# Block loads for k of chunk 2, v loaded and cast through GpSimd's queue, preparation ordered by tensor

## The chip, the cores and the metric

The kernel runs on one core of a Trainium2 chip. The metric is the time of one execution on the device, in microseconds; where several runs were made, their median is given. The core's engines are TensorE (PE, matrix products, with a weight load beside each), VectorE (DVE), ScalarE (ACT), GpSimd (POOL) and SyncE (SP). SP, ACT and GpSimd also issue DMA transfers, each through a queue of its own.

## What is computed

A retention layer (a linear recurrence with one decay per head) feeds a feed-forward layer with a tanh GELU:

```python
def _attn_ref(q, k, v):                       # B, H, S, D = 4, 8, 768, 64
    gamma = 1.0 - 2.0 ** (-5.0 - np.arange(H))
    state = zeros(B, H, D, D)
    for t in range(S):
        state = gamma * state + k[t] (outer) v[t]
        y[t] = (1/sqrt(D)) * q[t] @ state

def reference(q, k, v, moe_w_in, moe_w_out):
    x = attn_out.transpose(0, 2, 1, 3).reshape(B * S, H * D)   # 3072 x 512
    h = x @ w_in                                               # 512 x 2048
    return gelu_tanh(h) @ w_out                                # 3072 x 512
```

All inputs and the output are float32. The kernel computes in float16 with float32 accumulation.

## The kernel before

The sequence of 768 steps is cut into 6 chunks of 128, numbered 0 to 5. Within a chunk the recurrence becomes three matrix products for each of the 4 batches: scores (`mm_A`, k against q, masked by `ev_A`), the output inside the chunk (`mm_yi`, v against the masked scores) and the output from the state that the earlier chunks left (`mm_yc`). A fourth product, `mm_s`, makes the chunk's contribution to the state; `ev_S` adds it to the decayed state, and `decay` (on GpSimd) prepares the next decayed copy. The transposed result is copied to `xT` and feeds the feed-forward part of the same chunk: `moe1` (16 units with GELU on ScalarE), then `moe2` (4 batches of 4 units each, `units2`), whose results go out by `ev_O`.

**Order.** The order of the instructions on every engine is the order in which the program writes them; nothing reorders them. `run(units, after)` writes the units of TensorE work one after another and, after the unit of a given number, the extra calls listed under that number. So the attention work of chunk c+1 is threaded between the feed-forward units of chunk c. The phases from chunk 1 on are: `moe2` of chunk 0 with the transposes and scores of chunk 1; `moe1` of chunk 1 in halves (16 units) with loads, preparation and transposes of chunk 2; `moe2` of chunk 1; then a loop over c = 2, 3, 4 with one list of 32 units each, in which chunk n = c + 1 is prepared; at last chunk 5 alone.

**Loads and preparation.** `load(c)` writes the loads of a chunk to SP's queue. A tensor is loaded in one of two ways. `load1` (L102) brings 128 x 512 float32 of one batch with time on the partitions, in rows of 256 bytes. `load_blk` (L114) brings a tensor of all four batches in 16 DMAs of 64 KB with rows of 128 bytes, placed so that a transposition of each 32 x 32 block is all that is missing. `prep1` (L185, L188) multiplies q or k by its decay factors, or casts v; `prep_blk` (L199) does the same for the block form. `prep(c, b)` writes all of these for one batch to GpSimd.

**Transposes.** The scores need q and k with the head dimension on the partitions. What was loaded in block form is transposed by VectorE, 32 x 32 at a time (L251). The rest is transposed by TensorE against an identity matrix into PSUM (`mm_T`, L242) and copied to SBUF by `ev_T` (L226). Which tensor of which chunk takes which way is set by `BLK`: q from chunk 2 on, k from chunk 3 on. k also keeps its ordinary form, since `mm_s` needs it.

**Buffers.** Pools of tiles go round: a new tile takes the oldest buffer of its tag, and its first writer waits until the earlier readers are done. q's raw block tile has two buffers, that of k one (`kT32`); raw k and v have six each, the prepared block k (`kT16`) two.

A TensorE unit of `moe1` or `moe2` in the later phases is 4 matmuls. DMA issues by SP, ACT and GpSimd appear in the profile as DMA_DIRECT2D.

Of the kernel before, what the change touches and what calls it, by code (L numbers as in the profile page):

```python
# [9 lines left out]
F16 = mybir.dt.float16  # L10
F32 = mybir.dt.float32
# [5 lines left out]
def kernel(  # L17
# [9 lines left out]
    nc = tc.nc  # L27
    B, H, S, Dh = q.shape
    C = 128
    NCk = S // C  # L30
    NHP = H // 2
# [27 lines left out]
    ld = ctx.enter_context(tc.tile_pool(name="ld", bufs=2 * B))  # L59
    pre = ctx.enter_context(tc.tile_pool(name="pre", bufs=2 * B))  # L60
    att = ctx.enter_context(tc.tile_pool(name="att", bufs=4))
# [13 lines left out]
    raw = {}  # L75
# [1 line left out]

    BLK = {"q": (2, 3, 4, 5), "k": (3, 4, 5)}  # L80

    def ld_all(key):
        if key not in raw:
            raw[key] = ld.tile(
                [128, B * NHP, 4, 32],
                F32,
                tag=key[0],
                bufs=2 if key[0] == "q32" else 1,
                name=key[0],
            )  # L90
        return raw[key]

    def ld_tile(nm, c, b):
        if nm == "q":
            t = ld_all(("q32", c)).rearrange("p (b hp) a d -> p b (hp a d)", b=B)
            return t[:, b].rearrange("p (h d) -> p h d", h=H)
        if (nm, c, b) not in raw:
            raw[nm, c, b] = ld.tile([128, H, Dh], F32, tag=f"{nm}32", bufs=6, name=f"{nm}32")
        return raw[nm, c, b]

    def load1(eng, nm, c, b):
        eng.dma_start(  # L102
            out=ld_tile(nm, c, b),
            in_=srcs[nm][b, :, c * C:(c + 1) * C, :].rearrange("h p d -> p h d"),
        )

    def load_blk(nm, c):
        t = ld_all((nm + ("32" if nm == "q" else "T32"), c))
        src = srcs[nm].rearrange("b (hp j) s (dd d) -> j dd s (b hp) d", j=2, dd=2)
        for j in range(2):  # L110
            for dd in range(2):
                for a in range(4):
                    p0, t0 = (2 * j + dd) * 32, c * C + a * 32
                    nc.sync.dma_start(  # L114
                        out=t[p0:p0 + 32, :, a, :], in_=src[j, dd, t0:t0 + 32]
                    )

    def load(c):
        for nm in "qk":
            if c in BLK[nm]:  # L120
                load_blk(nm, c)
        for b in range(B):
            for nm in "vk" if c in BLK["k"] else "kv":
                load1(nc.sync, nm, c, b)

    def hold(nm, c, b, until):

# [18 lines left out]
        out=misc[:, 0:1], in_=zero[:, 0:1], func=AF.Gelu_apprx_tanh, scale=1.0  # L146
# [16 lines left out]
    for j in range(2):  # L163
        for hp in range(NHP):
            nc.vector.tensor_scalar(
                out=mask[:, j, hp],
# [6 lines left out]
    h16 = {}  # L173
    blk16 = {}

    def prep1(eng, nm, c, b):
        t = pre.tile(
            [128, H, Dh], F16, tag=f"{nm}16", bufs=6 if nm == "q" else 2 * B, name=f"{nm}16"
        )
        src = ld_tile(nm, c, b)  # L180
        if nm == "v":
            if eng is nc.scalar:
                eng.copy(out=t, in_=src)  # L183
            else:
                eng.tensor_copy(out=t, in_=src)  # L185
        else:
            col = OQ if nm == "q" else OK
            eng.tensor_tensor(  # L188
                out=t,
                in0=src,  # L190
                in1=cst[:, col:col + H].unsqueeze(2).broadcast_to([128, H, Dh]),
                op=ALU.mult,
            )
        h16[nm, c, b] = t

    def prep_blk(nm, c, b):
        key, tag, col = ("q32", "q16", OQT) if nm == "q" else ("kT32", "kT16", OKT)
        t = pre.tile([128, NHP * 4, 32], F16, tag=tag, bufs=6 if nm == "q" else 2, name=tag)
        nc.gpsimd.tensor_tensor(  # L199
            out=t,  # L200
            in0=ld_all((key, c))[:, b * NHP:(b + 1) * NHP].rearrange("p hp a d -> p (hp a) d"),
            in1=cst[:, col:col + 16].unsqueeze(2).broadcast_to([128, 16, 32]),
            op=ALU.mult,
        )
        blk16[nm, c, b] = t

    def prep(c, b):
        for nm in "qk":
            if c in BLK[nm]:
                prep_blk(nm, c, b)  # L210
        prep1(nc.gpsimd, "k", c, b)
        prep1(nc.gpsimd, "v", c, b)

    def pair(t, hp):
        return t[:, 2 * hp:2 * hp + 2]

    qkT = {}
    a_sb = {}
    xT = {}
    pss = {}  # L220

    def copy_on(eng, out, in_):
        if eng is nc.scalar:
            eng.copy(out=out, in_=in_)  # L224
        else:
            eng.tensor_copy(out=out, in_=in_)  # L226
# [5 lines left out]
    def bank(tag, dt=F32, shape=(128, NHP, 128), name="ps"):  # L232
        return psum.tile(list(shape), dt, tag=tag, bufs=BANKS[tag], name=name)

    def mm_T(c, b):
        parts = [(i, nm) for i, nm in enumerate("qk") if c not in BLK[nm]]
        if not parts:
            return
        ps = bank("att", F16, (128, 2, NHP, 128), "qkT_ps")
        for i, nm in parts:  # L240
            for hp in range(NHP):
                nc.tensor.transpose(  # L242
                    out=ps[:, i, hp], in_=pair(h16[nm, c, b], hp), identity=iden
                )
        pss["T", c, b] = ps

    def ev_T(c, b, eng=nc.vector):
        t = att.tile([128, 2, NHP, 128], F16, tag="qkT", name="qkT")
        for i, nm in enumerate("qk"):
            if c in BLK[nm]:  # L250
                nc.vector.transpose(  # L251
                    out=t[:, i].rearrange("p hp t -> p (hp t)"),
                    in_=blk16.pop((nm, c, b)).rearrange("p ha d -> p (ha d)"),
                )
        if ("T", c, b) in pss:
            i0 = sum(c in BLK[nm] for nm in "qk")
            copy_on(eng, t[:, i0:], pss.pop(("T", c, b))[:, i0:])
        qkT[c, b] = t

    def mm_A(c, b):  # L260
        t = qkT[c, b]
# [90 lines left out]
    def att_T(c, *bs):  # L352
        for b in bs:
            mm_T(c, b)
            ev_T(c, b)
# [73 lines left out]
    def moe1(c, fc):  # L429
        h_ps = bank("h", shape=(128, B * C), name="h_ps")  # L430
        moe1_mm(c, fc, h_ps, 0, B * C)
        gelu(g_tile(c, fc)[:, fc % 2], h_ps)
# [55 lines left out]
    def run(units, after):  # L488
        for i, u in enumerate(units):
            u()  # L490
            for f, *args in after.get(i, ()):
                f(*args)

    VE, AC, PO, SY = nc.vector, nc.scalar, nc.gpsimd, nc.sync
# [88 lines left out]
    def units2(c, b, n=4, tag="o"):  # L583
        u = [(lambda i=i: moe2(c, b, range(i, i + n), tag)) for i in range(0, NF, n)]
        last = u[-1]
        u[-1] = lambda: (last(), ev_O(c, b))
        return u
# [30 lines left out]


    load(2)  # L620
    for b in range(B):
        prep(2, b)
    run(
        [
            (lambda fp=fp, t=t: moe1_two(1, fp, *t))
# [2 lines left out]
        ],  # L628
        {
            1: [(att_AY, 1, (2,), "o", 1, (3,), VE)],  # L630
            3: [(att_S, 1, 2)],
            4: [(att_AY, 1, (3,), "o", 1, (), VE)],
            6: [(att_S, 1, 3)],
            8: [(att_T, 2, 0), (load, 3)],
            10: [(att_T, 2, 1)],
            12: [(att_AY, 1, (), "o", 2, (0, 1), None)],
            14: [(att_T, 2, 2)],
            15: [(att_T, 2, 3)],
        },
    )  # L640
    run(
        [x for b in range(B) for x in units2(1, b)],
        {
            2: [(att_AY, 2, (0, 1), "h", 2, (2, 3), AC)],
            4: [(att_S, 2, 0)],
            5: [(att_S, 2, 1)],
            8: [(att_AY, 2, (2, 3), "h", 2, (), AC)],
            10: [(att_S, 2, 2)],
            11: [(att_S, 2, 3)],
        },  # L650
    )


    for c in range(2, NCk - 1):
        n = c + 1
        after = {
            2: [(prep, n, 0)],
            4: [(prep, n, 1)],
            6: [(prep, n, 2), (att_T, n, 0)],
            8: [(prep, n, 3), (att_T, n, 1)],  # L660
            9: [(load, n + 1)] if n + 1 < NCk else [],
            12: [(att_AY, n, (), "att", n, (0, 1), None)],
            13: [(att_T, n, 2)],
            15: [(att_T, n, 3)],
            18: [(att_AY, n, (0, 1), "h", n, (2, 3), VE)],
            20: [(att_S, n, 0)],
            21: [(att_S, n, 1)],
            25: [(att_AY, n, (2, 3), "h", n, (), AC)],
            27: [(att_S, n, 2)],
            28: [(att_S, n, 3)],  # L670
        }
        run(
            [(lambda fc=fc: moe1(c, fc)) for fc in range(NF)]
            + [x for b in range(B) for x in units2(c, b)],
            after,
        )
    c = NCk - 1
# [36 lines left out]
```

## Time and profile before

| | |
|---|---|
| time, median of 10 runs | 217.9 us (216.68 to 218.16) |
| the profiled execution's own time | 218.05 us |
| its span, first to last instruction | 215.8 us |
| TensorE busy | 207.4 us (96%) |
| VectorE, ScalarE, GpSimd busy | 82.8, 87.2, 96.9 us |
| mean granted TensorE clock | 0.996 |
| DMA | 124417 packets, 32.88 MB, mean 152 GB/s |
| block loads of q, of kT | 64 and 48 DMAs of 64 KB, 2.8 and 2.7 us from issue to landing |
| k and v loads on SP | 22 and 18 DMAs of 256 KB, 4.6 and 4.3 us to landing |

The profile is of one execution. "Busy" counts an engine's own work and not its DMA issues by SP or its waits. Groups and waits are named by line number, engine, and the tiles written and read; a wait names the waiter, then who released it. Times within the execution are counted from the start of the span.

### The profile page before, as it was taken

The page shows a single profiled execution, that of the slowest core. Times are in us where ns is not written, and L with a number is a line of the kernel's source. Part 1 is how long each engine was busy: PE and PEld are TensorE (multiplying, and loading weights), DVE is VectorE, ACT ScalarE, POOL GpSimd, SP SyncE. Part 2 cuts the span into 40 slices and gives each one's busy share as a digit, 9 for nine tenths or more (in the row PEclk, how much of TensorE's full clock was granted, in tenths as well). Part 3 has the DMA queues.
Part 4 walks back from the last instruction along what each step waited for, and adds up shares of the span by engine and source line. Part 5 has one row for each costly group of instructions (what it writes and reads, how often), then busy time and mean ns, then how long its engine had stood idle before and what let it go on. Part 6 is the DMA issues. An engine that isn't in the chain of part 4 may idle for free.

```text
span 215.8 us, 3912 instructions
## 1 busy us (share of the span) xinstructions
PE 207.4 (96%) x1544; PEld 113.0 (52%) x1544; DVE 82.8 (38%) x152; ACT 87.2 (40%) x150; POOL 96.9 (45%) x116
## 2 busy tenths in 40 slices
PE   7889999999979999999999999999999999999993
PEld 2447644457867655444545444545444545444462
DVE  3445200198635562153691343682344650100001
ACT  2584562254444233276223275223366123476120
POOL 3599200324169542699433799412399321100000
PEclk9999999999999999999999999999999999999998
DMA  7999999997899789997679975589900012100111
GB/s 175 288 249 207 206 204 241 214 319 124 178 226 199 111 156 185 248 256 124 103 145 257 280 130 88 81 160 248 290 2 3 0 49 87 62 0 0 52 75 71
DMA packets 124417, 32.88 MB, mean 152 GB/s; under 512 B 118064, under 2 KB 122544, under 8 KB 124400
## 3 DMA queue, kind: packets, MB, share of 16 engines
q1 hardware_dynamic: 107984, 20.58, 48.3%
q0 software_dynamic: 5584, 8.65, 17.1%
q10 hardware_dynamic: 10832, 3.41, 6.5%
q8 instruction: 12, 0.20, 0.4%
q14 instruction: 5, 0.04, 0.1%
HBM read 30.53 MB, written 6.29 MB: 171 GB/s over the span
## 4 chain that ended last, share of the span: by engine, by line
PE 68%; DMA 15%; SPq 9%; POOL 5%; issue 1%; DVE 0%; ACT 0%
PE o_ps L445 32%; PE h_ps L412 28%; DMA w_out<-in_moe_w_out_dram 7%; DMA k<-in_k_dram 6%; SPq L102 5%; SPq L114 4%; PE y_ps L300 2%; PE a_ps L265 2%; POOL k L188 2%; PE y_ps L287 2%; DMA v<-in_v_dram 2%; PE s_ps L319 1%; POOL w_in L393 1%; POOL q L199 1%; POOL w_out L402 1%
## 5 line engine op out<-in xcount | busy, mean ns | idle before, releaser
L445 PE MATMUL o_ps<-w_out,g 128*128 128x512 f16 (+1 forms) x400 | 88.1, 371 | 0.0
L412 PE MATMUL h_ps<-xT,w_in 128*128 128x512 f16 (+2 forms) x488 | 86.6, 334 | 0.5 <-ACT g L427 0.5
L427 ACT ACTIVATE g<-h_ps 128x512 f16<-128x512 f32 (+1 forms) x98 | 57.4, 588 | 51.7 <-PE h_ps L412 51.7
L412 PEld LDWEIGHTS <-w_in 128*128 128x128 f16 x488 | 45.7, 98 | 37.0 <-issue 0.7
L445 PEld LDWEIGHTS <-g 128*128 128x128 f16 x400 | 37.7, 98 | 38.8
L278 DVE TENSOR_TENSOR a_sb<-a_ps,mask 128x512 f16<-128x512 f32 x48 | 30.1, 684 | 19.6 <-PE a_ps L265 19.5
L188 POOL TENSOR_TENSOR k<-k,cst 128x512 f16<-128x512 f32 x24 | 25.1, 1047 | 16.7 <-DMA k<-in_k_dram 16.7
L470 POOL DMA_DIRECT2D out_dram<-o_sb x17 | 9.7, 568 | 46.4 <-ACT o_sb L465 36.8
L465 ACT COPY o_sb<-o_ps 128x512 f32<-128x512 f32 x19 | 11.1, 585 | 42.5 <-PE o_ps L445 33.8
L345 POOL TENSOR_TENSOR stg<-st,cst 128x512 f32<-128x512 f16 x16 | 16.4, 1045 | 10.3 <-DVE st L336 9.3
L336 DVE TENSOR_TENSOR st<-s_ps,stg 64x256 f16<-64x256 f32 x32 | 13.5, 421 | 17.8 <-PE s_ps L319 17.2
L199 POOL TENSOR_TENSOR q<-q,cst 128x512 f16<-128x512 f32 x16 | 16.7, 1042 | 5.8 <-DMA v<-in_v_dram 5.8
L251 DVE STREAM_TRANSPOSE qkT<-q 128x512 f16<-128x512 f16 x16 | 11.2, 700 | 13.1 <-POOL q L199 13.1
L224 ACT CAST xT<-y_ps 128x512 f16<-128x512 f32 x15 | 8.3, 588 | 13.0 <-PE y_ps L300 12.9
L199 POOL TENSOR_TENSOR kT<-kT,cst 128x512 f16<-128x512 f32 x12 | 12.5, 1042 | 0.0
L188 DVE TENSOR_TENSOR q<-q,cst 128x512 f16<-128x512 f32 x7 | 4.8, 686 | 18.7 <-DMA q<-in_q_dram 18.7
L152 PE MATMUL spin_ps<-zero 128*128 128x512 f16 x32 | 10.4, 467 | 1.2 <-DVE zero L144 1.2
L482 DVE COPY o_sb<-o_ps 128x256 f32<-128x256 f32 x1 | 0.4, 424 | 25.2 <-PE o_ps L445 25.2
L185 POOL CAST v<-v 128x512 f16<-128x512 f32 x16 | 9.6, 601 | 0.0
L183 ACT CAST v<-v 128x512 f16<-128x512 f32 x8 | 5.0, 621 | 10.0 <-issue 7.7
L251 DVE STREAM_TRANSPOSE qkT<-kT 128x512 f16<-128x512 f16 x12 | 8.3, 690 | 1.7 <-POOL kT L199 1.7
L226 DVE CAST xT<-y_ps 128x512 f16<-128x512 f32 x9 | 5.9, 687 | 7.8 <-PE y_ps L300 7.8
(33 smaller groups left out, 97.1 us busy)
## 6 DMA issues: line engine op xcount, KB each, us to landing
k<-in_k_dram SPq DMA_DIRECT2D x22, 256.0 KB, 4.6
v<-in_v_dram SPq DMA_DIRECT2D x18, 256.0 KB, 4.3
out_dram<-o_sb POOLq DMA_DIRECT2D x17, 256.0 KB, 3.3
q<-in_q_dram SPq DMA_DIRECT2D x64, 64.0 KB, 2.8
kT<-in_k_dram SPq DMA_DIRECT2D x48, 64.0 KB, 2.7
w_in<-in_moe_w_in_dram POOLq DMA_DIRECT2D x4, 512.0 KB, 9.2
w_out<-in_moe_w_out_dram POOLq DMA_DIRECT2D x4, 512.0 KB, 14.6
v<-in_v_dram ACTq DMA_DIRECT2D x6, 256.0 KB, 5.9
```

What stands on the lines that cost most here:

```text
L102: eng.dma_start(out=ld_tile(nm, c, b), in_=srcs[nm][b, :, c * C:(c + 1) * C, :].rearrange("h p d -> p h d"),)
L152: nc.tensor.matmul(out=ps, lhsT=zero[:, 0:128], rhs=zero, start=True, stop=True)
L188: eng.tensor_tensor(out=t, in0=src, in1=cst[:, col:col + H].unsqueeze(2).broadcast_to([128, H, Dh]), op=ALU.mult,)
L199: nc.gpsimd.tensor_tensor(out=t, in0=ld_all((key, c))[:, b * NHP:(b + 1) * NHP].rearrange("p hp a d -> p (hp a) d"), in1=cst[:, col:col + ...
L251: nc.vector.transpose(out=t[:, i].rearrange("p hp t -> p (hp t)"), in_=blk16.pop((nm, c, b)).rearrange("p ha d -> p (ha d)"),)
L278: nc.vector.tensor_tensor(out=s, in0=ps[j], in1=mask[:, j], op=ALU.mult)
L336: eng.tensor_tensor(out=st[sl, :, b, sl], in0=s_ps[sl, :, sl], in1=stg[sl, :, b, sl], op=ALU.add,)
L345: nc.gpsimd.tensor_tensor(out=stg[:, :, b], in0=st[:, :, b], in1=cst[:, OG:OG + NHP].unsqueeze(2).broadcast_to([128, NHP, 128]), op=ALU.mult,)
L412: nc.tensor.matmul(out=out, lhsT=w_in_sb[wi][:, kc, wr * 128:(wr + 1) * 128], rhs=xT[c][:, kc, t0:t1], start=(kc == 0), stop=(kc == NHP - ...
L427: nc.scalar.activation(out=out, in_=in_, func=AF.Gelu_apprx_tanh, scale=1.0)
L445: nc.tensor.matmul(out=ps[:, n0:n1], lhsT=g_sb[c, fc // 2][:, fc % 2, b * C:(b + 1) * C], rhs=w_out_sb[fc // (NF // NO)][:, fc % (NF // NO ...
L465: nc.scalar.copy(out=o_sb, in_=ps)
```

## The change

- k of chunk 2 is loaded in block form too (`BLK`), so no chunk from 2 on is transposed by TensorE. `mm_T` and `ev_T` keep only the form for chunks 0 and 1.
- v of chunks 2 to 5 is no longer loaded as float32 by SP and cast by an instruction on GpSimd. `load_v` issues a DMA from GpSimd's queue that casts to float16 and writes the `v16` tile.
- `load` now issues q's blocks, kT's blocks, and then k in ordinary form, which is not loaded (or prepared) for the last chunk, whose state nobody needs.
- The raw block tiles of q and k have two buffers each; raw k and v have four.
- `prep` takes a tensor and a list of batches: `"Q"` and `"K"` for the block forms, `"k"` for the ordinary one. `tr` writes the VectorE transposes of one tensor. The calls are placed tensor by tensor, where before they were placed batch by batch.
- In the phase of `moe1` of chunk 1, the scores of chunk 2 for batches 0 and 1 move from its unit 12 to unit 3 of the next phase, those for batches 2 and 3 from unit 2 to unit 6 of that phase, and what follows moves by three units.

```diff
-    BLK = {"q": (2, 3, 4, 5), "k": (3, 4, 5)}
+    BLK = {"q": (2, 3, 4, 5), "k": (2, 3, 4, 5)}
...
-                bufs=2 if key[0] == "q32" else 1,
+                bufs=2,
...
-            raw[nm, c, b] = ld.tile([128, H, Dh], F32, tag=f"{nm}32", bufs=6, name=f"{nm}32")
+            raw[nm, c, b] = ld.tile([128, H, Dh], F32, tag=f"{nm}32", bufs=4, name=f"{nm}32")
...
         for nm in "qk":
             if c in BLK[nm]:
                 load_blk(nm, c)
+        if c + 1 < NCk:
+            for b in range(B):
+                load1(nc.sync, "k", c, b)
+
+    def load_v(c):
+
         for b in range(B):
-            for nm in "vk" if c in BLK["k"] else "kv":
-                load1(nc.sync, nm, c, b)
+            t = h16["v", c, b] = pre.tile([128, H, Dh], F16, tag="v16", bufs=2 * B, name="v16")
+            nc.gpsimd.dma_start(
+                out=t, in_=v[b, :, c * C:(c + 1) * C, :].rearrange("h p d -> p h d")
+            )
...
-    def prep(c, b):
-        for nm in "qk":
-            if c in BLK[nm]:
-                prep_blk(nm, c, b)
-        prep1(nc.gpsimd, "k", c, b)
-        prep1(nc.gpsimd, "v", c, b)
+    def prep(c, nm, *bs):
+
+        for b in bs:
+            if nm in "QK":
+                prep_blk(nm.lower(), c, b)
+            else:
+                prep1(nc.gpsimd, nm, c, b)
...
+    def tr(c, nm, *bs):
+        for b in bs:
+            if (c, b) not in qkT:
+                qkT[c, b] = att.tile([128, 2, NHP, 128], F16, tag="qkT", name="qkT")
+            nc.vector.transpose(
+                out=qkT[c, b][:, "qk".index(nm)].rearrange("p hp t -> p (hp t)"),
+                in_=blk16.pop((nm, c, b)).rearrange("p ha d -> p (ha d)"),
+            )
...
     load(2)
-    for b in range(B):
-        prep(2, b)
+    load_v(2)
     run(
...
             1: [(att_AY, 1, (2,), "o", 1, (3,), VE)],
-            3: [(att_S, 1, 2)],
+            3: [(att_S, 1, 2), (prep, 2, "Q", 0, 1, 2, 3)],
             4: [(att_AY, 1, (3,), "o", 1, (), VE)],
-            6: [(att_S, 1, 3)],
-            8: [(att_T, 2, 0), (load, 3)],
-            10: [(att_T, 2, 1)],
-            12: [(att_AY, 1, (), "o", 2, (0, 1), None)],
-            14: [(att_T, 2, 2)],
-            15: [(att_T, 2, 3)],
+            6: [(att_S, 1, 3), (tr, 2, "q", 0, 1, 2, 3)],
         },
     )
+    prep(2, "K", 0, 1, 2, 3)
+    prep(2, "k", 0, 1, 2, 3)
+    load(3)
+    load_v(3)
     run(
         [x for b in range(B) for x in units2(1, b)],
         {
-            2: [(att_AY, 2, (0, 1), "h", 2, (2, 3), AC)],
-            4: [(att_S, 2, 0)],
-            5: [(att_S, 2, 1)],
-            8: [(att_AY, 2, (2, 3), "h", 2, (), AC)],
-            10: [(att_S, 2, 2)],
-            11: [(att_S, 2, 3)],
+            2: [(tr, 2, "k", 0, 1)],
+            3: [(att_AY, 2, (), "att", 2, (0, 1), None), (tr, 2, "k", 2, 3)],
+            6: [(att_AY, 2, (0, 1), "h", 2, (2, 3), AC)],
+            8: [(att_S, 2, 0)],
+            9: [(att_S, 2, 1)],
+            11: [(att_AY, 2, (2, 3), "h", 2, (), AC)],
+            13: [(att_S, 2, 2)],
+            14: [(att_S, 2, 3)],
         },
     )
...
     for c in range(2, NCk - 1):
         n = c + 1
+        more = n + 1 < NCk
         after = {
-            2: [(prep, n, 0)],
-            4: [(prep, n, 1)],
-            6: [(prep, n, 2), (att_T, n, 0)],
-            8: [(prep, n, 3), (att_T, n, 1)],
-            9: [(load, n + 1)] if n + 1 < NCk else [],
+            1: [(prep, n, "Q", 0, 1, 2, 3), (tr, n, "q", 0, 1)],
+            6: [(prep, n, "K", 0, 1, 2, 3), (tr, n, "k", 0, 1), (tr, n, "q", 2, 3)],
+            10: [(prep, n, "k", 0, 1, 2, 3)] if n + 1 < NCk else [],
+            11: [(load, n + 1), (load_v, n + 1)] if more else [],
             12: [(att_AY, n, (), "att", n, (0, 1), None)],
-            13: [(att_T, n, 2)],
-            15: [(att_T, n, 3)],
+            13: [(tr, n, "k", 2, 3)],
             18: [(att_AY, n, (0, 1), "h", n, (2, 3), VE)],
```

## The prediction

> **What bounds the kernel now.** I read the busy table first, then the waits, the chain of waits, and the timelines of the engines around the one place where they point.
>
> ```profile
> span 215.8 us, 3912 instructions
> PE 207.4 (96%) x1544; PEld 113.0 (52%) x1544; DVE 82.8 (38%) x152; ACT 87.2 (40%) x150; POOL 96.9 (45%) x116
> ```
>
> TensorE sets the time: 96% busy, and no other engine reaches half. Only what it executes or waits for counts. Its largest wait (waiter, releaser, total, times, longest):
>
> ```profile
> PE qkT_ps L242 <- POOL k L188: 1.6, 2, 1.1
> ```
>
> That is 1.6 us in two stalls, in transposes of k that wait for GpSimd. The TensorE timeline puts both at chunk 2:
>
> ```profile
> 60.02 1.91 PE L412 MATMUL h_ps<-xT,w_in 128*128 128x256 f16 x16
> 63.07 0.40 PE L242 MATMUL qkT_ps<-iden,k 128*128 128x128 f16 x4 [1.14 <-POOL k L188]
> 63.30 1.91 PE L412 MATMUL h_ps<-xT,w_in 128*128 128x256 f16 x16
> 65.63 0.40 PE L242 MATMUL qkT_ps<-iden,k 128*128 128x128 f16 x4 [0.42 <-POOL k L188]
> ...
> 67.70 0.62 PE L265 MATMUL a_ps<-qkT 64*128 64x128 f16 x16
> ```
>
> TensorE stood from 61.93 to 63.07 and 0.42 us before 65.63. After 71.33 the chain runs on TensorE to the end with no such piece. What those stalls wait for, in the chain of waits:
>
> ```profile
> 57.50 3.47 DMA v<-in_v_dram
> 60.96 1.05 POOL q L199
> 62.01 1.00 POOL k L188
> ```
>
> and SP's own timeline:
>
> ```profile
> 46.12 10.80 SPq L114 DMA_DIRECT2D q<-in_q_dram  x16
> 56.96 0.49 SPq L102 DMA_DIRECT2D k<-in_k_dram  x1
> ...
> 74.85 9.21 SPq L114 DMA_DIRECT2D kT<-in_k_dram  x16
> ```
>
> Columns: start, duration, what. SP issues the 16 block loads of q, then k and v; they land; GpSimd prepares q, k, v of batch 0, and TensorE transposes. So the ground is SP's queue and the DMA engines. The last line prices 16 block loads: 0.58 us each.
>
> **What the Trainium skill says.** "DMA: Bandwidth & Descriptors", "Issuing engines are not separate DMA queues": transfers started by SP, ACT and GpSimd run on the same 16 DMA engines and interleave, so moving v to GpSimd's queue saves SP's issue time, not transfer time. The trace fits: mean DMA share is 0.93 from 57 to 64 us and 1.16 from 64 to 66, with all of it on SP's queue. Same page, "SWDGE vs HWDGE vs iDMA": a cast during a DMA needs GpSimd's queue, whose descriptors software writes. "SBUF — State Buffer", "Who interferes with whom": vector operations in a two-port mode lock GpSimd's descriptor writing out. Here the vector work beside the new loads is st, xT and a_sb out of PSUM or transposes at 0.69 us, which is the one-element-per-cycle pace of the same engine's other 512-wide work; the trace of before shows no such block.
>
> **The change, part by part.** All times are on the profiled execution (218.05 us, its span 215.8, so 2.25 around it); the median shown is 217.9, so a difference in the span is applied to 217.9.
>
> (a) Removed on TensorE: the 16 transposes of chunk 2's k. Each group of four costs the step from its start to the next work: 63.07 to 63.30, 65.63 to 65.86, 70.01 to 70.24, 71.11 to 71.33: 0.91 us. With them go the two stalls, 1.14 + 0.42 = 1.56. Together 2.47 us, all on the path: the most that this change can give.
>
> (b) Vector engine: four copies out of PSUM (0.40) become four transposes (0.69): +1.2 us, on an engine 38% busy; hidden, but see (e).
>
> (c) GpSimd: per chunk four v casts (4 x 0.60 = 2.4 us) become four DMA issues. A 128-row out issue takes 0.57, a 512-row weight issue 0.80; a v load has 1024 rows of 256 B, so the straight line through both gives an estimate of 1.1 us, 4.4 for four. Bounds: 0.57 if rows cost nothing; above, see rival 2. Chunk 2 also gains four kT preparations (4 x 1.04), chunk 5 loses its four k ones. In each 32 us chunk GpSimd then has 4.2 + 4.2 + 4.2 (q, kT, k), 4.4 (v), 2.3 (outs), 4.2 (decay): 23.5 us, so it keeps up.
>
> (d) SP: in the load of chunk 2, four v loads go and 16 block loads of kT come right behind q's, ahead of k. From 56.96, at 0.53 each (as SP issued them from 51 to 53 us), the last is issued by 65.4; landing 2.6 us after an issue near 64.9: 67.5. That is the best case. But the v loads, issued on GpSimd from 55.2 (its decay of 54.16 ends there) to 59.6, share the DMA engines. SP's k and v loads went at 8 in 8.25 us with the engines full, so v is about 4.1 us of all 16. The 19 block loads in that stretch take 0.27 us each (pace 0.53 at a share of 0.5, 51 to 53 us) to 0.41 (0.58 at 0.7, 72 to 78 us), 5.1 to 7.8 us. Sum 9 to 12 us in the 12 us from 55.2: nearly full. From 46.12 to 50.70, with other transfers ahead, SP managed only five block loads, 0.92 each. At that pace for all 16 and 4.8 us to land (the slowest kT), the last lands at about 75.6: the worst case. I take issue finished at 67.2 (1.8 us beyond the best), last issue at 66.7, and 3.5 us to land (the last two of q took 3.1 and 4.1): L = 70.2.
>
> (e) The new wait. Scores of chunk 2 (L265 before) now need the vector transposes of kT: L, two preparations (2.03), transpose (0.75 with its handover), 0.1 for semaphores: batch 1 can start at L + 2.87. TensorE gets there at 61.93 + 7 units of moe1 (1.75 per two, 6.13) + 4 units of moe2 (0.865, 3.46) = 71.5, and batch 1's scores 0.27 later, 71.77. The stall is L - 68.9, so 1.3 us. Queued behind it is everything on TensorE. Next, batches 2 and 3: the vector engine does four a_sb (2.45) and only then their two transposes (1.35); TensorE needs the last one 3 units + 0.45 + 0.27 after its scores, that is some 0.3 us too early: another 0.3 lost. GpSimd's third kT preparation waits for the first transpose (two buffers), which is done by then.
>
> (f) Further down. k of chunk 2 follows kT on SP: issued by 71.5, landed by about 76, prepared behind kT at 77 to 78.5, used by the first state update at about 79.8: hidden by about 4 us (first batch ready by 75.5). Chunk 3: SP then has 16 + 16 blocks, 71.5 + 9.6 + 9.2 + 1.5 (v of chunk 3 beside them) = 91.8, landed 94.5, scores possible at 97.4; TensorE gets there at about 88 + 13 units (11.2) = 99. Cover 1.7 us; from chunk 4 on SP is a whole chunk ahead, since the second kT buffer removes its waits. Preparing by tensor puts q and kT first (8.3 us after GpSimd is free at about 89), against scores 11 us into the chunk: hidden. The v16 and k32 buffers that the loads wait for are free long before.
>
> Sum: -2.47 + 1.3 + 0.3 = -0.87 us: 217.9 becomes **217.0 us**.
>
> **Rivals.** *1. The transfer is hidden anyway.* If the last kT lands before 68.9, only the 0.3 stays: -2.17, 215.7. For it: the DMA share leaves room on paper (9 of 12 us), and SP itself is the pacer at 0.53. Against it: landings stretch to 4.0 to 4.5 us whenever 256 KB loads run beside blocks, as at the end of chunk 3's kT.
>
> *2. GpSimd becomes the bound (slower).* The v issues stand ahead of q's and kT's preparation: 55.2 + 4t + one decay + four q + one decay + two kT + the transpose = 64.3 + 4t against 71.77. It decides from t = 1.9, eats the whole gain of 2.17 at t = 2.4, and at t = 3.1 ("SBUF — State Buffer", "A bandwidth-pool intuition that's wrong (but worth ruling out)", gives about 3100 ns for such a DMA beside a vector copy, 620 alone; taking it as the issue is an estimate) the scores start at 76.7: a stall of 4.9, +2.7, 220.6. Against it: issues in this trace never passed 0.93 us. For it: none has 1024 rows, nor a cast with rows that short.
>
> *3. The two queues share badly.* If v's packets get more than half of the engines, kT lands at 71.7 or later: a stall of 2.8, +0.6 or more; at 73, +1.9, 219.8. Break-even is L = 71.07.
>
> *4. Chunk 3 is late too.* If its blocks land 2.5 us later than I put them, its scores stall 0.8: -0.1, 217.8. That the transposes stay on TensorE is excluded by the code.
>
> **How the numbers follow.** A run of this kernel varies by about 0.3% (0.65 us), so less than that is called the same. Forecast, L from 69.0 to 71.4: 0.50, of which 0.33 is faster by more than 0.65 (L below 70.4) and 0.17 within it. Rival 1: 0.17, faster. Rival 2: 0.12, slower. Rival 3: 0.12, of which 0.03 same. Rival 4: 0.09, of which 0.07 same and 0.02 slower. That gives faster 0.50, same 0.27, slower 0.23. The range from 215.8 to 219.0 leaves out part of rival 1's lower end and the heavier ends of rivals 2 and 3, about 2 in 10; the forecast's own range is 215.8 to 218.2.
>
> **What would show it.** Right: no L242 work for chunk 2 and its two stalls gone; a wait of 1 to 2 us of the scores on the vector transpose of kT near 72, a smaller one some 4 us later; v issues on GpSimd of about 1.1 us; kT of chunk 2 issued until about 67. Wrong: issues of 2 us or more; block loads at 0.9 us each to the end; a wait at chunk 3's scores near 99; or TensorE work apart from chunk 2 that grew.

## The result

The changed kernel is slower: 219.44 us in the median of 14 runs (217.79 to 220.99) against 217.73 us of the kernel before (51 runs, 216.43 to 218.55). The ratio over these runs is 1.0086, with a 95% interval from 1.0067 to 1.0104 (that of the two medians alone is 1.0079). The forecast was 217.0 us, in a range from 215.8 to 219.0. Executions more than 1.5% above the fastest of their kernel are left out as slow, here and below: one of the changed kernel (222.09 us) and three of a later one.

The profiled execution of the changed kernel took 219.45 us, 1.40 more than that of before (218.05), and its span is 1.9 us longer. The head of its page:

```profile
span 217.7 us, 3866 instructions
PE 206.3 (95%) x1528; PEld 112.1 (51%) x1528; DVE 84.2 (39%) x152; ACT 87.0 (40%) x150; POOL 102.2 (47%) x116
```

TensorE has 16 matmuls fewer and 1.1 us less to do, as meant, and yet the span grew: TensorE waits more than it saves. The waits of the changed kernel (waiter, releaser, total, times, longest) say for what:

```profile
PE a_ps L271 <- DVE qkT L261: 3.1, 3, 1.9
```

The two stalls of the transposes of k, 1.6 us, are gone. Three new ones, 3.1 us, stand at the scores, which wait for VectorE's transposes of kT. TensorE's timeline (start, duration, work, and in brackets the idle time ahead) has two of these waits at chunk 2 and the third at chunk 3:

```profile
73.42 0.40 PE L271 MATMUL a_ps<-qkT 64*128 64x128 f16 x8 [1.92 <-DVE qkT L261]
74.43 0.40 PE L271 MATMUL a_ps<-qkT 64*128 64x128 f16 x8 [0.61 <-DVE qkT L261]
...
88.85 11.39 PE L418 MATMUL h_ps<-xT,w_in 128*128 128x512 f16 x52
100.31 0.40 PE L271 MATMUL a_ps<-qkT 64*128 64x128 f16 x8
101.31 0.40 PE L271 MATMUL a_ps<-qkT 64*128 64x128 f16 x8 [0.61 <-DVE qkT L261]
101.64 2.55 PE L418 MATMUL h_ps<-xT,w_in 128*128 128x512 f16 x11
```

and the same two places in the kernel before:

```profile
88.83 11.39 PE L412 MATMUL h_ps<-xT,w_in 128*128 128x512 f16 x52
...
100.70 2.76 PE L412 MATMUL h_ps<-xT,w_in 128*128 128x512 f16 x12
```

Two readings settle where the time went. At 88.85 against 88.83 the changed kernel is exactly level: the saved 2.47 us have been paid back by 1.92 + 0.61 = 2.53 us of waiting. At 101.64 against 100.70 it is 0.94 us behind; 0.61 of that is shown as a wait of the second half of the scores. Nothing of size follows: the last block of `moe2` starts at 199.11 us against 198.02, 1.09 later, and takes 14.02 us in both. What is left of the longer span is its tail, the landing of the last output (2.6 us against 2.0), far from anything that the change touches.

What the scores waited for is seen in GpSimd's and SP's timelines. GpSimd:

```profile
55.16 3.56 POOL L130 DMA_DIRECT2D v<-in_v_dram  x4
...
71.57 4.07 POOL L207 TENSOR_TENSOR kT<-kT,cst 128x512 f16<-128x512 f32 x4 [4.57 <-DMA k<-in_k_dram]
...
79.58 3.57 POOL L130 DMA_DIRECT2D v<-in_v_dram  x4
...
98.46 4.06 POOL L207 TENSOR_TENSOR kT<-kT,cst 128x512 f16<-128x512 f32 x4 [3.68 <-DMA kT<-in_k_dram]
```

SP:

```profile
57.09 11.76 SPq L114 DMA_DIRECT2D kT<-in_k_dram  x16
...
82.42 13.55 SPq L114 DMA_DIRECT2D kT<-in_k_dram  x16
```

GpSimd stood idle for 4.57 and 3.68 us for want of kT. It was free; the data was not there. (The releaser given for the first is a k load that landed at about that time; by the code the instruction needs kT.) The 16 block loads of kT took SP 11.76 us in chunk 2, 0.74 each, and 13.55 in chunk 3, 0.85 each, where those of chunk 3 took 9.21 before, 0.58 each. In both chunks they began before GpSimd had issued the last of its four v loads. A table by stretches, from 60 to 63 us (PE, PEld, DVE, ACT and POOL busy, the clock, the mean DMA share, GB/s), first after the change, then before:

```profile
60.00:63.00 3.00, 3.00 (x32) 2.69 (x30) 0.84 (x2) 1.94 (x4) 1.06 (x2) 1.00 2.06 161
```

```profile
60.00:63.00 3.00, 1.93 (x20) 1.49 (x17) 1.56 (x3) 1.78 (x3) 2.04 (x3) 1.00 0.87 198
```

The share more than doubles, from 0.87 to 2.06, while the GB/s fall from 198 to 161. The two stretches carry different loads (k and v in rows of 256 bytes before; blocks and v, counted by its written float16 bytes, after), so the lines say no more than this: the share counts how long packets last, not how much the engines move. It passes 1 also where only SP's queue is at work, as the prediction noted (1.16 from 64 to 66 us before).

How SP's pace changes is plainer. The four v loads of chunk 2 land between 60.26 and 64.22 us. Up to 64.11 us SP gets seven blocks of kT out in 6.97 us, 1.00 each; the nine after that take 4.74 us, 0.53 each. In chunk 3 the v loads have landed at 88.46, and the blocks come back to 0.53 only from 92.30 on; stores of the output run beside them there too, so not all of that chunk's delay need be v's.

### The profile page after: what moved, and what is told of

Its sections match the earlier page's. It is cut to its first block, busy times and chain, and to the rows that moved or that the text cites. A ratio compares the mean times of both kernels' runs of the same rounds, so it can differ in the third digit from the quotient of the medians.

```text
span 217.7 us, 3866 instructions
## 1 busy us (share of the span) xinstructions
PE 206.3 (95%) x1528; PEld 112.1 (51%) x1528; DVE 84.2 (39%) x152; ACT 87.0 (40%) x150; POOL 102.2 (47%) x116
## 3 DMA queue, kind: packets, MB, share of 16 engines
q10 hardware_dynamic: 10832, 3.41, 6.5%
## 4 chain that ended last, share of the span: by engine, by line
PE 51%; SPq 25%; DMA 14%; POOL 4%; issue 3%; DVE 0%; ACT 0%; POOLq 0%
PE o_ps L451 26%; PE h_ps L418 20%; SPq L114 19%; DMA w_out<-in_moe_w_out_dram 7%; SPq L102 6%; DMA k<-in_k_dram 6%; PE y_ps L306 2%; PE a_ps L271 1%; DMA kT<-in_k_dram 1%; PE y_ps L293 1%; POOL w_in L399 1%; PE s_ps L325 1%; POOL k L196 1%; POOL kT L207 1%; POOL w_out L408 1%
## 5 line engine op out<-in xcount | busy, mean ns | idle before, releaser
L476 POOL DMA_DIRECT2D out_dram<-o_sb x17 | 9.7, 574 | 40.5 <-ACT o_sb L471 32.7
L196 POOL TENSOR_TENSOR k<-k,cst 128x512 f16<-128x512 f32 x20 | 20.7, 1050 | 16.7 <-DMA k<-in_k_dram 16.7
L207 POOL TENSOR_TENSOR kT<-kT,cst 128x512 f16<-128x512 f32 x16 | 16.2, 1043 | 8.2 <-DMA k<-in_k_dram 4.6
L261 DVE STREAM_TRANSPOSE qkT<-kT 128x512 f16<-128x512 f16 x16 | 10.9, 697 | 17.7 <-POOL kT L207 17.7
L207 POOL TENSOR_TENSOR q<-q,cst 128x512 f16<-128x512 f32 x16 | 16.2, 1049 | 2.2 <-DMA kT<-in_k_dram 2.1
L130 POOL DMA_DIRECT2D v<-in_v_dram x16 | 14.3, 912 | 0.0
L233 ACT CAST xT<-y_ps 128x512 f16<-128x512 f32 x15 | 8.3, 588 | 14.3 <-PE y_ps L306 14.2
L271 PE MATMUL a_ps<-qkT 64*128 64x128 f16 x192 | 8.5, 218 | 3.7 <-DVE qkT L261 3.1
L160 PE MATMUL spin_ps<-zero 128*128 128x512 f16 x32 | 9.9, 448 | 1.2 <-DVE zero L152 1.2
```

The lines of the kernel that those rows point to most:

```text
L130: nc.gpsimd.dma_start(out=t, in_=v[b, :, c * C:(c + 1) * C, :].rearrange("h p d -> p h d"))
L196: eng.tensor_tensor(out=t, in0=src, in1=cst[:, col:col + H].unsqueeze(2).broadcast_to([128, H, Dh]), op=ALU.mult,)
L207: nc.gpsimd.tensor_tensor(out=t, in0=ld_all((key, c))[:, b * NHP:(b + 1) * NHP].rearrange("p hp a d -> p (hp a) d"), in1=cst[:, col:col + ...
L261: nc.vector.transpose(out=qkT[c, b][:, "qk".index(nm)].rearrange("p hp t -> p (hp t)"), in_=blk16.pop((nm, c, b)).rearrange("p ha d -> p ( ...
```

## The experiments

Three theories of why the blocks of kT come late were to be told apart. A: the casting load through GpSimd's queue is itself what is heavy. B: any v transfer that runs beside the blocks holds them back by about what it takes itself, whoever issues it and in whatever form. C: SP's own 16 further blocks are what is late, and v has no part. For A speaks the list of DMA queues (packets, MB, share of 16 engines' span):

```profile
q0 software_dynamic: 22224, 10.75, 31.6%
```

Before it is 5584 packets, 8.65 MB and 17.1%. The v loads add 16640 packets of 128 written bytes, which last (0.316 x 217.7 - 0.171 x 215.8) x 16 = 510 us in sum, 31 ns each. That is 2.0 us of all 16 engines per load, 8 per chunk, twice the 4.1 that the prediction took.

**v as float32 through ACT's queue, cast by GpSimd**

```diff
 def load_v(c):  # the calls are spread over ACT's work
-    nc.gpsimd.dma_start(out=t, in_=v[b, :, ...])      # t: float16
+    load1(nc.scalar, "v", c, b)                       # float32, 8 buffers
 ...
+    (prep, 2, "v", 0, 1, 2, 3)                        # casts, behind prep of q (chunk 2), of kT (later)
```

> The changed kernel, but v of chunks 2 to 5 comes as float32 through ACT's queue at about the times at which GpSimd's queue issued it, and GpSimd casts it by instruction. Theory A (the v loads that cast cost the DMA engines about 31 ns a packet where an ordinary 256-byte packet costs 15 to 20, and that slows the block loads of kT): block loads of chunk 2 are issued by about 67 us instead of 68.9, the wait of chunk 2's scores falls from 2.5 to about 1.2 us, the wait of chunk 3's scores (0.9) goes, and the time is about 217.0 (0.3% below the kernel before). Theory B (any second queue beside SP's block loads slows them as much, cast or not): nothing changes, 219.4. Theory C (SP's own queue with 16 more block loads is what is late, v has no part): also 219.4, with block loads at the same pace.

Measured: 228.62 us, ratio 1.051 (1.0445 to 1.0576). A miss for all theories, and of little use for telling them apart. SP's waits show why:

```profile
SPq L114 <- DMA v<-in_v_dram: 32.7, 10, 8.4
```

SP's block loads waited 32.7 us for v loads that ACT issues between its other work, so the 16 blocks of q of chunk 3 took SP 19.50 us. Two queues that were meant to be apart hung together through the waits that the program puts ahead of a DMA: a block of q went out at 57.53 us, when the v load that ACT had issued at 54.11 had landed (57.51). Where v was not in the way, the blocks of kT of chunk 2 went out in 8.51 us, 0.53 each: the pace without company.

**v as float32 through GpSimd's queue, cast by GpSimd**

```diff
-    nc.gpsimd.dma_start(out=t, in_=v[b, :, ...])      # t: float16
+    load1(nc.gpsimd, "v", c, b)                       # float32, 8 buffers
 ...
+    (prep, 2, "v", 0, 1, 2, 3)                        # casts, places as above
```

> The changed kernel, but v comes as float32 through GpSimd's queue (no cast in the DMA), and GpSimd casts it by instruction. This separates the cast from the queue. Theory A with the cast as the cost: packets of queue 0 cost under 20 ns for v, and the time is that of the run with ACT's queue, about 217.0. Theory A' (the cost comes with GpSimd's software queue, not with the cast): v packets still cost about 31 ns, and the waits are those of the changed kernel, 219.4. GpSimd has 2.4 us more work in each chunk, which has cover in both.

Measured: 221.01 us, ratio 1.0136 (1.0106 to 1.0167), above both times that were expected; part of the excess over the changed kernel is a lower clock behind its long wait (last section). Its queue line and its block loads of kT for chunks 2 and 3:

```profile
q0 software_dynamic: 6864, 12.85, 22.9%
```

```profile
57.80 12.51 SPq L114 DMA_DIRECT2D kT<-in_k_dram  x16
...
83.95 13.84 SPq L114 DMA_DIRECT2D kT<-in_k_dram  x16
```

Without the cast the same v takes 1280 packets in place of 16640 and about 0.8 us of packet time per load in place of 2.0, (0.229 x 219.0 - 0.171 x 215.8) x 16 / 16 loads / 16 engines. Yet the blocks are as slow: 12.51 and 13.84 us. A falls: neither the cast nor the number of v's packets is the cause, and packet time was no measure of what v takes from others. What the expectation calls A', that the cost comes with GpSimd's queue as such, does not fall: the run with ACT's queue was to tell it from B, and could not.

**v of chunks 3 to 5 issued behind kT's preparation**

```diff
-    load_v(3)                                         # with load(3)
 ...
-    6: [(prep, n, "K", 0, 1, 2, 3), (tr, n, "k", 0, 1), ...],
+    6: [(prep, n, "K", 0, 1, 2, 3), (load_v, n), (tr, n, "k", 0, 1), ...],
-    11: [(load, n + 1), (load_v, n + 1)] if more else [],
+    11: [(load, n + 1)] if more else [],
```

> The changed kernel, but the casting v loads of chunks 3, 4 and 5 are issued after the preparation of kT of the same chunk, so that none runs beside the block loads of kT of chunk 3. The same transfers, at another time. Theory A or B: the block loads of kT of chunk 3 return from 0.85 us each to about 0.6, the wait of chunk 3's scores (0.9 us) goes, that of chunk 2 stays at 2.5, and the time falls by about 0.9 to 218.5. Theory C: chunk 3's blocks are as slow as before, 219.4.

Measured: 220.49 us, ratio 1.0113 (1.0046 to 1.0179): not faster than the changed kernel, where 218.5 was expected. Its mechanism is as expected. SP, and TensorE at chunk 3:

```profile
84.41 9.39 SPq L114 DMA_DIRECT2D kT<-in_k_dram  x16
```

```profile
101.01 0.62 PE L271 MATMUL a_ps<-qkT 64*128 64x128 f16 x16
```

With v out of the way the same 16 loads take 9.39 us, not 13.55, GpSimd starts on kT at 96.62 and not at 98.46, and chunk 3's scores don't wait. v's delay moves to the blocks of q of chunk 4 (12.23 us, not 9.48), for which nothing waits. But at chunk 2, where v was left as it is, the wait in this execution is 2.40 + 0.61 us, 0.48 more than in the changed kernel, so `moe1` goes on at 101.57 against 101.64. The execution shown took 219.5 us, and the four runs spread from 218.97 to 221.98, the upper two with a mean clock of 0.984; the mechanism is settled by this run, a gain in time is not.

**The kernel before with v alone moved to GpSimd's queue**

```diff
-        for nm in "vk" if c in BLK["k"] else "kv":
-            load1(nc.sync, nm, c, b)
+        load1(nc.sync, "k", c, b)
+def load_v(c):                                         # as in the changed kernel
...
-        prep1(nc.gpsimd, "v", c, b)
```

> The kernel before with one part of the change alone: v of chunks 2 to 5 through GpSimd's queue with the cast, and no cast instruction. Chunk 2's k still goes through TensorE. Theory A: k of chunk 2 lands later because v's loads run beside it, so TensorE's stall before its first transpose grows from 1.1 to about 2 us, partly given back by SP's four loads fewer: 217.7 to 218.7. Rival (moving v off SP is a gain by itself, because SP's queue and GpSimd's work are shorter): the stalls of 1.6 us shrink, 216.5.

Measured: 222.02 us, ratio 1.0168 (1.0107 to 1.0229), 3.9 us slower than before (218.12 beside it) and beyond the 218.7 that was expected at most. SP's k loads and TensorE:

```profile
57.45 8.60 SPq L102 DMA_DIRECT2D k<-in_k_dram  x4
```

```profile
65.99 0.61 PE L247 MATMUL qkT_ps<-iden,k 128*128 128x128 f16 x4 [3.69 <-POOL k L194]
66.40 3.62 PE L417 MATMUL h_ps<-xT,w_in 128*128 128x256 f16 x16
```

SP has half the DMAs of before and is no quicker: four k loads take 8.60 us, 2.15 each, where eight of k and v took 8.25 on one queue. So moving v is costly also where no blocks of kT run beside it. The stall grows from 1.14 to 3.69 us. It is not the whole loss: at 73.17 us the kernel is 4.92 us behind the one before (68.25), of which 2.13 are longer stalls and some 2.4 are work at a lower clock. (The 3.62 us for work that takes 1.91 is the subject of the last section.)

**v as float32 on SP's queue, behind kT and ahead of k**

```diff
 def load(c):  # behind the block loads
+    for b in range(B):
+        load1(nc.sync, "v", c, b)
-    load_v(c)                                         # everywhere
+    prep(c, "v", 0, 1, 2, 3)                          # casts, behind prep of kT
```

> The changed kernel, but v of chunks 2 to 5 comes as float32 on SP's own queue, behind kT and ahead of k, and GpSimd casts it by instruction after kT. No second queue runs beside the block loads. Theory B (a v transfer on any second queue beside the block loads slows them, cast or not): chunk 2's kT is issued by about 66 us and landed by 68.5, the wait of chunk 2's scores (2.5 us in the changed kernel) goes, a wait of up to 0.6 may come where chunk 2 first uses v, chunk 3 waits for nothing: about 216.3. Theory C (the 16 further block loads on SP are late by themselves): kT of chunk 2 still lands near 71, and the time stays at 219.4 or above, since SP has four loads more per chunk.

Measured: 218.36 us in the median of 17 runs (217.62 to 220.50), ratio 1.0033 (1.0008 to 1.0057). The changed kernel's loss is mostly gone, but the 216.3 that was expected did not come. Twelve of the runs, with a mean clock of 0.996 or more, have a median of 217.83, where the kernel before took 218.07 beside them; the other five, with 0.988 to 0.990, took 219.73 to 220.50. SP, GpSimd's line for kT of chunk 2, and TensorE:

```profile
56.74 9.07 SPq L114 DMA_DIRECT2D kT<-in_k_dram  x16
65.86 3.25 SPq L102 DMA_DIRECT2D v<-in_v_dram  x4
69.20 4.35 SPq L102 DMA_DIRECT2D k<-in_k_dram  x4
```

```profile
68.39 4.07 POOL L201 TENSOR_TENSOR kT<-kT,cst 128x512 f16<-128x512 f32 x4 [3.88 <-DMA v<-in_v_dram]
```

```profile
71.59 0.62 PE L265 MATMUL a_ps<-qkT 64*128 64x128 f16 x16
...
99.03 0.40 PE L265 MATMUL a_ps<-qkT 64*128 64x128 f16 x8 [1.17 <-DVE qkT L255]
```

(The releaser given on GpSimd's line is a v load; by the code the instruction needs kT, whose last block landed at 67.99.) Chunk 2 is as the change meant it: kT is ready at 68.39, and the scores wait for nothing. SP spends 9.07 + 3.25 us on kT and v, one behind the other; together they end at 69.11, where in the changed kernel, on two queues, SP is done with kT alone at 68.85. From the first issue of the two to the last landing it is 15.95 us here (56.74 to 72.69) and 16.02 on two queues (55.16 to 71.18). The second queue didn't shorten the whole; v's time came out of kT's. But v and k, 7.6 us of SP, now stand ahead of chunk 3's blocks, and the wait comes back there, 1.17 us and then another 0.61. Of 2.4 us gained at chunk 2, 0.3 is left at chunk 3 (`moe1` goes on at 100.37 against 100.70).

**The changed kernel without v of chunks 2 to 5**

```diff
-            t = h16["v", c, b] = pre.tile(...)
-            nc.gpsimd.dma_start(out=t, in_=v[b, :, ...])
+            h16["v", c, b] = h16["v", 1, b]
```

> The changed kernel without the v loads of chunks 2 to 5: those chunks use chunk 1's v tiles instead, so that part of the computation is not the reference's, and everything else stays. It takes the suspected traffic away altogether. Theory B: block loads go at 0.53 to 0.6 us throughout, kT of chunk 2 lands by 68.5, no wait at the scores of chunks 2 and 3, and the time is 215.7 (the whole 2.47 us of removed work and stalls, less 0.3). Theory C: the waits stay, 219.4 or little less.

Measured: 215.96 us (215.77 to 216.74), ratio 0.9911 (0.9883 to 0.994); 215.7 was expected. SP's blocks of kT for chunks 2 and 3, GpSimd at chunk 2, and TensorE:

```profile
57.27 9.36 SPq L114 DMA_DIRECT2D kT<-in_k_dram  x16
...
80.78 10.81 SPq L114 DMA_DIRECT2D kT<-in_k_dram  x16
```

```profile
68.99 4.07 POOL L204 TENSOR_TENSOR kT<-kT,cst 128x512 f16<-128x512 f32 x4 [3.29 <-DMA kT<-in_k_dram]
```

```profile
86.26 11.39 PE L415 MATMUL h_ps<-xT,w_in 128*128 128x512 f16 x52
97.58 0.62 PE L268 MATMUL a_ps<-qkT 64*128 64x128 f16 x16
98.13 2.76 PE L415 MATMUL h_ps<-xT,w_in 128*128 128x512 f16 x12
```

Take v's transfers away and everything that the change was to bring is there: `moe1` of chunk 2 starts at 86.26, 2.57 us earlier than before, there is no wait at either chunk, and the lead is still 2.57 at 98.13. v's transfers cost some 3.5 us (219.44 - 215.96), more than the whole loss of 1.7. kT comes 2.58 us earlier than in the changed kernel (68.99 against 71.57). GpSimd's issues of v are gone too, but it stands idle for kT here as well (3.29 us), so they were not what held it. C falls: all blocks are still on SP, and in time. B holds for v on GpSimd's queue, with or without the cast; that any other queue would do the same is not shown.

**The kernel before with k ahead of v on SP, and ahead of q on GpSimd, in chunk 2**

```diff
+        if c == 2:
+            for nm in "kv":
+                for b in range(B):
+                    load1(nc.sync, nm, c, b)
+            return
...
     for b in range(B):
-        prep(2, b)                                    # q, k, v of one batch after another
+        prep1(nc.gpsimd, "k", 2, b)
+        prep_blk("q", 2, b)
+    for b in range(B):
+        prep1(nc.gpsimd, "v", 2, b)
```

> The kernel before, with one change of order: in chunk 2, SP loads the four k ahead of the four v, and GpSimd prepares k ahead of q for each batch and casts v last. If TensorE's 1.6 us of stalls at chunk 2 stand for the order on GpSimd and SP, the first falls from 1.1 to about 0.4 us and the second goes: 216.8. If they stand for when the transfers land, nothing changes: 217.9. It tells what the place is worth without the block loads and without v's new queue.

Measured: 216.75 us (216.31 to 217.26), ratio 0.9947 (0.9923 to 0.997), where 216.8 was expected. TensorE:

```profile
62.87 0.40 PE L247 MATMUL qkT_ps<-iden,k 128*128 128x128 f16 x4 [0.54 <-POOL k L193]
...
64.87 0.40 PE L247 MATMUL qkT_ps<-iden,k 128*128 128x128 f16 x4
```

Of the stalls of 1.14 and 0.42 us, 0.54 and 0 are left. Putting what is waited for ahead of what is not, in two queues, takes most of the stall away with no new instruction and no byte more; this version beats both kernels.

**The changed kernel with eight matmuls on zeros ahead of chunk 2's scores**

Some runs of the changed kernel and its variants have a lower mean clock, so I asked whether the clock, and not the wait, makes the median slow. TensorE was to be kept busy through most of the 1.92 us wait.

```diff
-            3: [(att_AY, 2, (), "att", 2, (0, 1), None), ...],
+            3: [(spin, 8), (att_AY, 2, (), "att", 2, (0, 1), None), ...],
```

> The changed kernel with eight matmuls on zeros (about 1.7 us on TensorE, their result not used) just ahead of chunk 2's first scores, where TensorE waits for 1.9 us in the profile. If long waits also lower TensorE's granted clock for some us afterwards (as seen in three other runs after waits of 3 us and more), and that is what spreads the changed kernel's times from 217.8 to 221, then filling the wait costs nothing and takes the slow runs away: median about 218.9, with a narrower spread and a clock of 0.997 or more in every run. If the clock has no part in it, the median stays at 219.4 with the same spread.

Measured: 219.81 us (219.32 to 221.6), ratio 1.007 (1.0043 to 1.0097); 218.9 was expected. A miss. In the profiled execution kT was ready 1.22 us later than in the changed kernel (72.79), so 1.46 us of wait were left behind the zeros, and the clock fell all the same (last section). The changed kernel's own runs answer the question better: nine of the 14 have a mean clock of 0.994 or more and a median of 219.29; the other five, with 0.991 or 0.992, took 219.66 to 220.99. So a lower clock goes with the upper part of the spread, but the nine alone are 1.56 us above the kernel before: the clock does not make the loss.

## Why the prediction was wrong

**(a), the gain, right.** Predicted 2.47 us; 2.57 appear in the run without v.

**(b) and (c), right.** Neither VectorE nor GpSimd became the bound. A v issue takes 0.91 us (16 issues, 14.3 us), where 1.1 was taken and 1.9 was the point from which it decides: rival 2 didn't come. VectorE is 39% busy.

**(d), the step that failed: what v beside the blocks costs them.** It has two parts. (L is taken here as GpSimd's start on kT; the last block landed 0.39 us ahead of it, with v and without.) The floor, L = 67.5 with the blocks at 0.53 each, was too early: even without v the blocks go at 9.36 / 16 = 0.585, and kT is ready at 68.99. And v comes on top with 2.58 us (71.57 - 68.99), where the 2.7 between the floor and my 70.2 was to cover both. Behind it is a wrong reading of the DMA share. I added v's engine time to that of the blocks, found 9 to 12 us of demand in 12, and let v run largely in what the blocks left free. A share of 0.5 beside a pace of 0.53 is not half a machine left over. With v, the share rose past 2 and the blocks slowed from 0.585 to 0.74 each; the run with v on SP shows kT and v taking 16 us from first issue to last landing, the same as on two queues. The Trainium skill, "DMA: Bandwidth & Descriptors", "Queues, rings and completion order", says that a DMA engine takes turns between the queues that have work, a packet at a time. That fits the blocks' slower pace beside either form of v, but no run here shows the order of packets, so it stays an argument.

**(e), its formula right, its input wrong.** The stall was to be L - 68.9. With the true L it is 2.67; measured 2.53. With kT at 68.99 in the run without v, it is nothing, as measured. The further 0.3 us at batches 2 and 3 didn't come: no wait stands there. So chunk 2 came out at -2.47 + 2.53, level, which is rival 3 at about its break-even (71.07 with the 0.3, 71.4 without).

**(f), the same failure again.** Between 71.5 and the end of kT's issues of chunk 3 I put 20.3 us, 1.5 of it for v. Measured: 72.24 to 95.97, 23.7 us. v's part is 13.55 - 9.39 = 4.2 us by the run with v late, 2.7 by the run without v (10.81). kT was ready at 98.46, not 94.5: 4.0 late. The cover was 1.7, and 1.3 more since TensorE had gained nothing at chunk 2; 4.0 - 3.0 = 1.0 us, and the measured delay is 0.94. This is rival 4.

**The sum.** -2.47 + 2.53 + 0.94 = +1.00, and 1.09 at the last block of `moe2`. The own times differ by 1.40 and the medians by 1.71; what lies between 1.09 and 1.71 is partly the tail and partly the five runs of lower clock (without them the medians differ by 1.56), and for the rest not explained.

**The chances.** Rivals 3 and 4 were given 0.12 and 0.09, each with the other at rest. They have one cause, v beside the blocks, which acts in every chunk. As one case, by my own numbers, they give -2.47 + 2.8 + 0.3 + 0.8 = +1.4, or 219.3: above the range, and close to what was measured. That sum was not made.

## What to carry to other kernels

Moving a transfer to another engine's queue did not take it out of the way. As a first estimate, take the whole of what it lasts on one queue (here 3.25 us for 1 MB) as delay of whatever runs beside it (measured here: 2.58 us in chunk 2, 2.7 to 4.2 in chunk 3), and add that to each wait in each stage that it touches, as one case. Before another path is built for late data, look at what stands ahead of it in its queue: here a change of order in two queues won 1.2 us (0.53%) at no cost, while new loads, a second copy of k among them, brought new waits. A mean DMA share is no measure of room; the pace of the same loads with and without company is.

## What the runs showed of the hardware

A long wait of TensorE cost more than itself. In the run with v alone moved, the 16 matmuls behind the 3.69 us wait took 3.62 us in place of 1.91. In the run with v in float32 through GpSimd:

```profile
75.38 0.40 PE L268 MATMUL a_ps<-qkT 64*128 64x128 f16 x8 [3.64 <-DVE qkT L258]
...
76.92 4.03 PE L448 MATMUL o_ps<-w_out,g 128*128 128x512 f16 x12
```

Twelve matmuls that take 2.76 us elsewhere (with v on SP, from 72.15 us) take 4.03, at a granted clock of 0.50 for some 3 us. The Trainium skill, "TensorE: Matmul & The Clock Gate", "Part 1: The HAM clock gate", says that the clock halves after an idle window of about 3.4 us; the waits of 3.64 and 3.69 agree with that in length, and the waits of 1.92 + 0.61 and 2.40 + 0.61, after which nothing slowed, do too. Two cases don't fit: 3.06 + 0.49 us with v on ACT's queue, shorter than the window in each piece, was followed by 12 matmuls in 3.74 us, and in the last run above the clock fell after waits of only 1.46 + 0.61 us:

```profile
71.30 1.89 PE L160 MATMUL spin_ps<-zero 128*128 128x512 f16 x8
74.64 0.40 PE L271 MATMUL a_ps<-qkT 64*128 64x128 f16 x8 [1.46 <-DVE qkT L261]
...
75.98 4.45 PE L451 MATMUL o_ps<-w_out,g 128*128 128x512 f16 x12
```

That matmuls on zeros raise the clock is seen at the head of the changed kernel's trace: from 1.19 us TensorE has nothing else to do, one of them starts every 0.43 us up to 4.58 us and every 0.22 us from 4.97 us on, and the granted clock is 1.0 from 4.92 us.

The clock records show one thing more. In the four traces in which the clock fell during the work, it stayed at 0.50 for 3.41 us (twice for 6.83), and each fall lies a whole number of 3.41 us behind the first rise: 71.68 us, 21 steps, in the run with zeros and 68.27 us, 20 steps, with v on ACT's queue. So in these runs the clock changed only at fixed steps, and where a wait lies in a step may matter. With v on ACT's queue the step ahead of the fall, 71.60 to 75.01 us, holds all 3.06 us of the wait. In the run with zeros the step is 73.48 to 76.89 us: the zeros had ended at 73.19, ahead of it, and TensorE was idle for about 1.8 us of it. With v alone moved it was idle for about 2.2 us of the step ahead of the fall. But with v late a step with about 2.0 us of idle time (70.43 to 73.84) brought no fall. What decides is open.

Also new to me was that a casting load writes rows of 128 bytes one packet each (1040 packets for one v load, counted from the queue list, at 31 ns), while the same load without a cast is joined into 80 packets; and that the blocks beside it were as slow either way (12.51 us without the cast, 11.76 with it).
